# Local attention and a softplus FFN on one core: a hand-written issue order replaced by a list scheduler, with filler matmuls at the start

## Chip, cores and metric

The kernel runs on one core of a Trainium2 chip. The metric is the time of one execution on the device in microseconds (us); less is better. The profiler also gives the span, from the first to the last instruction, which is a little shorter.

## What is computed

Four batches, eight heads, 768 positions, head size 64. A query sees the first 8 keys of its batch and the 96 keys up to its own, with a bias that falls with the distance; softmax follows; the eight heads side by side are a row of 512 that goes through two matrices with a softplus between them:

```python
scores = scale * np.matmul(q, k.transpose(0, 1, 3, 2)) + bias[None, :, :, :]
scores = np.where(keep, scores, -1000000000.0)
a = np.exp(scores - np.max(scores, axis=-1, keepdims=True))
a = a / (np.sum(a, axis=-1, keepdims=True) + 1e-09)
attn_out = np.matmul(a, v)
x = attn_out.transpose(0, 2, 1, 3).reshape(B * S, H * D)    # 3072 x 512
h = x @ w_in                                                # w_in 512 x 2048
g = np.maximum(h, 0.0) + np.log1p(np.exp(-np.abs(h)))
out = g @ w_out                                             # w_out 2048 x 512
```

## The kernel before

**Units of work.** A *block* n (24 of them) is 128 positions of one batch with all heads. A *window* w (12) is two blocks: its q, k and v are loaded and transposed together. A *group* g (12) is the same 256 positions in the FFN. A group has eight *slots* p, each of two of the 16 chunks of the inner dimension.

**Attention of a window.** `load` (L96) fetches q, k, v in float32 on SyncE's queue, v in four pieces. `cast` (L114) makes bfloat16 of them (q on VectorE, k and v on GpSimd in most windows) and, for v, sets a column of ones with a memset (L130). `transp` (L133) has TensorE transpose q or k in eight steps into one PSUM bank `tr_ps` and copies them out on VectorE (L149).

**Attention of a block.** `scores` (L211) runs 16 small matmuls per half of the heads (8 in the first block of a batch) into `s_ps`, and VectorE adds the bias into `z` (L222). `expo` (L225) is ScalarE's exp. `pv` (L232) multiplies with v and the column of ones into `x_ps`, and VectorE normalizes into `xs` (L252, L253). `globals_k` on GpSimd (L160) and `globals_v` on VectorE (L167) copy the eight global keys and values into the neighbour block's tile, from block 2 of a batch on. `xs` then goes, transposed, to `XT`: for blocks 0 to 7 by TensorE and a copy (`x_transp`, L260), from block 8 on by a transposing DMA on SyncE's queue (`x_transp_dma`, L269). The first four blocks use `early_scores` (L191): there TensorE adds the bias, with matmuls of the bias by the identity (L196), and ScalarE reads PSUM directly. In these blocks the banks that later belong to the FFN serve as second banks for scores, for pv and for transposes (`s_alt`, `x_alt`, `tr_alt`, L399 to L402).

**FFN.** `mm1(g, p)` (L275) is eight matmuls of 256 columns into one of two banks `h_ps`, then an exp on ScalarE (L293) and, every second slot, one Ln with a bias of 1 over both slots (L295): softplus. `mm2(g, p)` (L302) is four matmuls of 512 columns into the two banks `o_ps`; after the last slot VectorE copies both banks (L316) and SyncE stores them (L320). `mm2` runs a group behind `mm1`.

**Weights.** `w_in_slice(s)` (L322) and `w_out_slice(s)` (L329) load a quarter of each matrix, with a cast to bfloat16, on GpSimd's DMA queue; a quarter serves two slots. `after_weights(s)` (L336) puts a tiny DMA on SyncE's queue that waits for a quarter of w_in, and so holds back the loads behind it.

**Order.** Every engine runs its instructions in the order in which the builder emits them. `at(t, fn, ...)` (L412) collects emissions with a time, and L544 sorts them. Up to about 49 us the times are written out one by one (L417 to L493); after that they follow from the block number, with a slot of 2.07 (L495 to L542). A `transp` emits its copy with it, a `scores` its bias add, a `pv` its normalization, an `mm1` its exp and Ln.

Of the kernel before, what the change touches and what calls it, by code (L numbers as in the profile page):

```python
# [12 lines left out]
BF16 = mybir.dt.bfloat16  # L13


@with_exitstack
def kernel(
# [19 lines left out]
    W = 2 * P  # L37
# [15 lines left out]
    GH = NG // 2  # L53

# [10 lines left out]
    ring = ctx.enter_context(tc.tile_pool(name="ring", bufs=5))  # L65
# [3 lines left out]

    s_ps = ps.tile([P, 8, P], F32, name="s_ps")  # L70
    x_ps = ps.tile([P, 512], F32, name="x_ps")
    tr_ps = ps.tile([P, 1024], BF16, name="tr_ps")
# [11 lines left out]

    state = {}

    def raw_tiles(w):
        if ("raw", w) not in state:
            state["raw", w] = (
                raw.tile([P, H, 2 * D], F32, tag="q32", name="q32"),  # L90
                raw.tile([P, H, 2 * D], F32, tag="k32", name="k32"),
                raw.tile([P, 2, H, D], F32, tag="v32", name="v32"),
            )
        return state["raw", w]

    def load(w, what, heads=slice(0, H)):  # L96
        b, ww = divmod(w, WPB)
        sl = slice(W * ww, W * ww + W)
        q32, k32, v32 = raw_tiles(w)
        if what == "v":  # L100
            for blk in range(2):
                t0 = W * ww + P * blk
                vv = v[b, :, t0 : t0 + P, :].rearrange("h (p r) d -> r p h d", r=2)
                for r in range(2):
                    nc.sync.dma_start(v32[64 * r : 64 * r + 64, blk, :, :], vv[r])  # L105
        else:
            dst, src = (q32, q) if what == "q" else (k32, k)
# [4 lines left out]
    cast_on = {"pool": nc.gpsimd.tensor_copy, "dve": nc.vector.tensor_copy, "act": nc.scalar.copy}  # L112

    def cast(w, which, eng, hs=slice(0, H)):  # L114
        q32, k32, v32 = raw_tiles(w)
        copy = cast_on[eng]
        if which in "qk":
            src = q32 if which == "q" else k32
            if (which + "b", w) not in state:
                state[which + "b", w] = qkv.tile(  # L120
                    [P, 2, H, D], BF16, tag=which + "b", name=which + "b"
                )
            copy(  # L123
                state[which + "b", w][:, :, hs, :],
                src[:, hs, :].rearrange("p h (r d) -> p r h d", r=2),
            )
        else:
            t = ring.tile([P, 2, H, D + 1], BF16, tag="vb", name="vb")
            copy(t[:, :, :, 0:D], v32[:])
            nc.gpsimd.memset(t[:, :, :, D : D + 1], 1.0)  # L130
            state["vb", w] = t

    def transp(w, which, psum, eng, ms=range(NPAIR)):  # L133
        src = state[which + "b", w]
        key = (which + "T", w)
        if key not in state:
            state[key] = (ring if which == "k" else qkv).tile(
                [P, 2, NPAIR, 2, 64], BF16, tag=which + "T", name=which + "T"
            )
# [9 lines left out]
        cast_on[eng](  # L149
            state[key][:, :, lo : lo + n, :, :].rearrange("p b m r t -> p b (m r) t"),  # L150
# [3 lines left out]
    def kt_of(n):  # L154
        return state["kT", n // 2][:, n % 2, :, :, :].rearrange("p m r t -> p m (r t)")

    def vb_of(n):
        return state["vb", n // 2][:, n % 2, :, :]
# [14 lines left out]
    def score_matmuls(n, half, banks, begin):  # L173

        i = n % NBLK
        qT = state["qT", n // 2][:, n % 2, :, :, :].rearrange("p m r t -> p m (r t)")
        for lh in range(4):
            h = 4 * half + lh
            m, sub = h // 2, h % 2
            rows = slice(64 * sub, 64 * sub + 64)  # L180
            for b in range(1 if i == 0 else 2):
                j = lh // 2 if i == 0 else 2 * (lh // 2) + b
                nc.tensor.matmul(  # L183
                    banks[lh % 2][:, j, :],
                    kt_of(n - b)[rows, m, :],
                    qT[rows, m, :],
                    start=begin,
                    stop=begin or (lh >= 2 and b == (0 if i == 0 else 1)),
                )

    def early_scores(n, half, banks):  # L191
# [11 lines left out]
        score_matmuls(n, half, banks, False)  # L203
        pb = work.tile([P, 8, P], BF16, tag="pb", name="pb")
        for e in range(2):
            nc.scalar.activation(  # L206
                pb[:, nr * e : nr * e + nr, :], banks[e][:, 0:nr, :], AF.Exp, scale=1.0 / root_d
            )
        state["pb", n, half] = pb

    def scores(n, half):  # L211
        score_matmuls(n, half, [s_ps[:, 0:4, :], s_ps[:, 4:8, :]], True)
        z = work.tile([P, 8, P], F32, tag="z", name="z")
# [9 lines left out]
        state["z", n, half] = z  # L223

    def expo(n, half):  # L225
        nr = 4 if n % NBLK == 0 else 8
        z = state.pop(("z", n, half))
        pb = work.tile([P, 8, P], BF16, tag="pb", name="pb")
        nc.scalar.activation(pb[:, 0:nr, :], z[:, 0:nr, :], AF.Exp, scale=1.0 / root_d)  # L229
        state["pb", n, half] = pb  # L230

    def pv(n, half, psum):  # L232
        i = n % NBLK
        pb = state.pop(("pb", n, half))
        if half == 0:
            state["xs", n] = work.tile([P, H, D], BF16, tag="xs", name="xs")
        xs = state["xs", n]
        xv = psum[:, 0 : 4 * (D + 1)].rearrange("p (h e) -> p h e", e=D + 1)
        for lh in range(4):
            h = 4 * half + lh  # L240
            j = perm.index(lh)
            if i == 0:
                nc.tensor.matmul(xv[:, lh, :], pb[:, j, :], vb_of(n)[:, h, :])
            else:
                nc.tensor.matmul(  # L245
                    xv[:, lh, :], pb[:, 2 * j, :], vb_of(n)[:, h, :], start=True, stop=False
                )
                nc.tensor.matmul(  # L248
                    xv[:, lh, :], pb[:, 2 * j + 1, :], vb_of(n - 1)[:, h, :], start=False, stop=True
                )  # L250
# [9 lines left out]
    def x_transp(n, psum, eng):  # L260
        xs = state.pop(("xs", n))
        tr = psum[:, 0:512].rearrange("p (m t) -> p m t", m=NPAIR)
        for m in range(NPAIR):
            nc.tensor.transpose(
                tr[:, m, :], xs[:, 2 * m : 2 * m + 2, :].rearrange("p a b -> p (a b)"), ident[:]
            )
        cast_on[eng](XT[:, :, P * n : P * n + P], tr)

    def x_transp_dma(n):  # L269
        xs = state.pop(("xs", n))  # L270
        nc.sync.dma_start_transpose(
            XT[:, :, P * n : P * n + P], xs[:].rearrange("p h d -> p (h d)")
        )

    def mm1(g, p):  # L275
        hv = h_ps[state["hslot"]][:].rearrange("p (j t) -> p j t", j=2)
        state["hslot"] ^= 1
# [10 lines left out]
        if p % 2 == 0:  # L288
            state["e", g] = ffn.tile([P, 2, 512], F32, tag="e", name="e")
        if p == 0:  # L290
# [290 lines left out]
```

## Time and profile before

| | us |
|---|---|
| median of 3 runs | 256.09 |
| the runs | 254.40, 256.09, 257.31 |
| profiled execution, its own time | 257.29 |
| its span | 255.5 |
| TensorE busy in it | 224.9 (88%) |
| ScalarE busy | 155.0 (61%) |
| VectorE busy | 125.1 (49%) |
| GpSimd busy | 36.3 (14%) |

The profiled execution took 1.79 us more than its span. Its own time lies 1.20 us above the median. Busy time is that of instructions; TensorE's matmuls overlap, and an end of a matmul is modelled, so spacing from start to start tells more than a duration.

### The profile page before, as it was taken

Reading aid. Unit: us, or ns where it says so; the run is one execution under the profiler, and the core shown is the slowest. Engines: PE = TensorE matmul, PEld = TensorE weight load, DVE = VectorE, ACT = ScalarE, POOL = GpSimd, SP = SyncE. Lnnn points to the kernel's source line nnn. Section 1 sums busy time; section 2 is a strip of 40 time slices with the busy share of each in tenths; the row PEclk is TensorE's granted clock in tenths of the full one; section 3 lists DMA queues with packets and bytes.
Section 4 is the critical chain, followed back from the end, with each engine's and each line's share of the span. In section 5 each row is a group of like instructions: output and inputs, shape, how many; then the busy total and the mean of one; then the engine's idle time right before and its main releaser. Section 6 shows DMA issues by size and latency. Waiting matters only on the chain.

```text
span 255.5 us, 5108 instructions
## 1 busy us (share of the span) xinstructions
PE 224.9 (88%) x2096; PEld 149.5 (59%) x2096; DVE 125.1 (49%) x259; ACT 155.0 (61%) x207; POOL 36.3 (14%) x68
## 2 busy tenths in 40 slices
PE   2759885977599799599999999999999999999991
PEld 1335664654367466367667766766676667666540
DVE  7263404664544666544555675745656656420102
ACT  3564576772705657447767776777677777776600
POOL 3370070030311000401000301301003000000000
PEclk9997999999959999889999999999999999999998
DMA  6979999928990305913653842844633213113033
GB/s 184 269 119 196 238 153 180 267 47 212 278 251 3 82 3 126 246 23 82 175 139 81 241 106 41 234 103 129 164 82 66 61 21 85 22 26 79 0 82 83
DMA packets 67193, 31.80 MB, mean 124 GB/s; under 512 B 35425, under 2 KB 64097, under 8 KB 67169
## 3 DMA queue, kind: packets, MB, share of 16 engines
q1 hardware_dynamic: 62944, 27.27, 42.7%
q0 software_dynamic: 4224, 4.19, 10.7%
q8 instruction: 16, 0.26, 0.4%
q14 instruction: 9, 0.07, 0.1%
HBM read 27.26 MB, written 6.29 MB: 131 GB/s over the span
## 4 chain that ended last, share of the span: by engine, by line
PE 80%; DMA 6%; DVE 4%; ACT 3%; issue 2%; SPq 2%; POOL 1%; DVEq 0%; POOLq 0%
PE h_psa L281 18%; PE o_psc L307 17%; PE h_psb L281 16%; PE o_psd L307 16%; PE s_ps L183 5%; PE tr_ps L144 4%; DMA w_in_bf<-in_moe_w_in_dram 3%; DMA XT<-xs 2%; ACT g L295 2%; DMA v_84<-in_v_dram 2%; PE x_ps L245 2%; PE x_ps L248 2%; DVE z L222 1%; ACT e L293 1%; SPq L105 1%
## 5 line engine op out<-in xcount | busy, mean ns | idle before, releaser
L281 PEld LDWEIGHTS <-w_in_bf 128*128 128x128 bf16 x768 | 73.2, 99 | 26.2 <-issue 3.9
L307 PE MATMUL o_psc<-w_out_bf,g 128*128 128x512 bf16 x192 | 58.5, 387 | 5.1 <-ACT g L295 4.8
L307 PE MATMUL o_psd<-w_out_bf,g 128*128 128x512 bf16 x192 | 57.8, 383 | 0.0
L307 PEld LDWEIGHTS <-g 128*128 128x128 bf16 x384 | 35.6, 99 | 35.1 <-ACT g L295 5.6
L281 PE MATMUL h_psa<-XT,w_in_bf 128*128 128x256 bf16 x384 | 51.9, 280 | 4.2 <-DMA XT<-xs 3.0
L222 DVE TENSOR_TENSOR z<-s_ps,biasA 128x1024 f32<-128x1024 f32 x34 | 41.5, 1221 | 22.5 <-PE s_ps L183 22.2
L293 ACT ACTIVATE e<-h_psb 128x512 f32<-128x512 f32 x48 | 28.6, 597 | 38.0 <-PE h_psb L281 38.0
L295 ACT ACTIVATE g<-e 128x1024 bf16<-128x1024 f32 x48 | 50.8, 1057 | 1.5
L281 PE MATMUL h_psb<-XT,w_in_bf 128*128 128x256 bf16 x384 | 50.0, 273 | 0.0
L293 ACT ACTIVATE e<-h_psa 128x512 f32<-128x512 f32 x48 | 28.4, 591 | 35.0 <-PE h_psa L281 34.8
L229 ACT ACTIVATE pb<-z 128x1024 bf16<-128x1024 f32 (+1 forms) x40 | 39.3, 982 | 1.9 <-DVE z L222 1.5
L252 DVE RECIPROCAL rcp<-x_ps 128x4 f32<-128x4 f32 x46 | 8.2, 178 | 30.7 <-PE x_ps L248 26.4
L316 DVE COPY osb<-o_psc 128x512 f32<-128x512 f32 x12 | 8.3, 691 | 26.2 <-PE o_psc L307 25.8
L253 DVE TENSOR_TENSOR xs<-x_ps,rcp 128x256 bf16<-128x256 f32 x46 | 19.5, 425 | 1.6
L165 POOL COPY kT<-kT 128x32 bf16<-128x32 bf16 x16 | 3.4, 213 | 116.0 <-PE s_ps L183 116.0
L183 PEld LDWEIGHTS <-kT 64*128 64x128 bf16 x352 | 10.5, 97 | 14.9 <-issue 11.5
L183 PE MATMUL s_ps<-qT,kT 64*128 64x128 bf16 x336 | 18.2, 225 | 1.0 <-DVE kT L149 0.6
L149 DVE COPY qT<-tr_ps 128x1024 bf16<-128x1024 bf16 (+1 forms) x12 | 7.8, 646 | 22.4 <-PE tr_ps L144 22.4
L245 PE MATMUL x_ps<-vb,pb 128*128 128x65 bf16 x156 | 15.0, 194 | 1.6 <-ACT pb L206 1.0
L144 PE MATMUL tr_ps<-ident,qb 128*128 128x128 bf16 x88 | 7.7, 235 | 8.9 <-POOL qb L123 5.0
L248 PE MATMUL x_ps<-vb,pb 128*128 128x65 bf16 x156 | 15.1, 194 | 0.0
L245 PEld LDWEIGHTS <-pb 128*128 128x128 bf16 x160 | 12.7, 99 | 2.8 <-ACT pb L206 1.3
(90 smaller groups left out, 149.4 us busy)
## 6 DMA issues: line engine op xcount, KB each, us to landing
out_dram<-osb SPq DMA_DIRECT2D x48, 128.0 KB, 2.4
w_in_bf<-in_moe_w_in_dram POOLq DMA_DIRECT2D x4, 512.0 KB, 7.3
w_out_bf<-in_moe_w_out_dram POOLq DMA_DIRECT2D x4, 512.0 KB, 9.7
q_82<-in_q_dram SPq DMA_DIRECT2D x2, 256.0 KB, 3.7
k_83<-in_k_dram SPq DMA_DIRECT2D x2, 256.0 KB, 4.1
v_84<-in_v_dram SPq DMA_DIRECT2D x4, 128.0 KB, 4.3
q_93<-in_q_dram SPq DMA_DIRECT2D x1, 512.0 KB, 4.9
k_94<-in_k_dram SPq DMA_DIRECT2D x1, 512.0 KB, 6.1
```

What stands on the lines that cost most here:

```text
L144: nc.tensor.transpose(tr[:, m - lo, r, :], src[:, r, 2 * m : 2 * m + 2, :].rearrange("p a b -> p (a b)"), ident[:],)
L183: nc.tensor.matmul(banks[lh % 2][:, j, :], kt_of(n - b)[rows, m, :], qT[rows, m, :], start=begin, stop=begin or (lh >= 2 and b == (0 if i ...
L222: nc.vector.tensor_tensor(z[:], s_ps[:], biasA[:, half, :, :], ALU.add)
L229: nc.scalar.activation(pb[:, 0:nr, :], z[:, 0:nr, :], AF.Exp, scale=1.0 / root_d)
L245: nc.tensor.matmul(xv[:, lh, :], pb[:, 2 * j, :], vb_of(n)[:, h, :], start=True, stop=False)
L248: nc.tensor.matmul(xv[:, lh, :], pb[:, 2 * j + 1, :], vb_of(n - 1)[:, h, :], start=False, stop=True)
L253: nc.vector.tensor_tensor(xs[:, 4 * half : 4 * half + 4, :], xv[:, :, 0:D], rcp[:][:, :, None].to_broadcast([P, 4, D]), ALU.mult,)
L281: nc.tensor.matmul(hv[:, j, :], w_in_bf[:, m, fb * P : fb * P + P], XT[:, m, W * g : W * g + W], start=(m == 0), stop=(m == NM - 1),)
L293: nc.scalar.activation(e[:, p % 2, :].rearrange("p (j t) -> p j t", j=2), hv, AF.Exp)
L295: nc.scalar.activation(state["g", g][:, 2 * p - 2 : 2 * p + 2, :].rearrange("p a t -> p (a t)"), e[:].rearrange("p a t -> p (a t)"), AF.Ln ...
L307: nc.tensor.matmul(o_ps[ns][:], gt[:, fb, ns * P : ns * P + P], w_out_bf[:, fb, :], start=(fb == 0), stop=(fb == NFB - 1),)
L316: nc.vector.tensor_copy(osb[:], o_ps[ns][:])
```

## The change

All work is described to a `Planner` as operations: engine (or a choice of engines), rough duration, what it comes after, the buffers that it takes and frees, and a rank. `plan` plays the program: whenever an engine is free in the play, it takes the operation of lowest rank whose inputs are done and whose buffers are free. The sequence so found is the order of emission. The play counts a result as seen 0.22 us after TensorE's end and 0.1 us after that of another engine, and models all DMAs as one pipe, first come, first served (1.85 us for q or k of a window, 2.45 for v, 3.1 for a weight slice, 0.65 for a transposing DMA, 0.7 to land). Semaphores are still placed by what an instruction reads and writes; the play decides the order alone.

With it: the functions are split, so that a copy, bias add, exp, Ln, normalization or store can stand elsewhere than right behind its matmuls. While TensorE has nothing ready before 24.0 in the play and bank pair O is free, a filler (identity by identity, 128 columns, into bank d) is emitted every 0.1. Weight slices 0 and 1 are planned from the landing of window 1's q on, slices 2 and 3 from that of window 2's q on; a DMA gate after slice 1 stands ahead of window 2's loads (as before) and one after slice 3, where it was slice 2, ahead of window 3's. Ranks put attention of block n (from 4 on) at 4n - 11 and `mm1` of group g at 8g, in slots. Blocks 6 and 7 use the transposing DMA. In the early blocks pv has one bank; q of window 1 is cast on GpSimd and k on ScalarE (before the other way round). The v tiles are five fixed ones, with their ones set once at the start. The last group's first output copy is on ScalarE. The arithmetic is the same.

The diff, cut; the removed functions and times are in the listing above:

```diff
--- before.py
+++ after.py
...
+    SEEN = {"pe": 0.22, "dve": 0.1, "act": 0.1, "pool": 0.1, "sp": 0.0}
...
+            for e in engine_free:
+                while engine_free[e] <= now:
+                    skipped, picked = [], None
+                    q = waiting[e]
+                    while q:
...
+                        if len(taken) == len(op.takes):
+                            picked = op
+                            break
+                        skipped.append(item)
...
+                    op = picked
+                    for b, slot in taken:
+                        self.rings[b][slot] = False
+                        self.turn[b] = (slot + 1) % len(self.rings[b])
+                    op.start, op.on, op.taken = now, e, taken
+                    engine_free[e] = op.end = now + op.engines[e]
+                    if op.dma is not None:
+                        first = now + 1.3 if e == "sp" else op.end + 1.2
+                        pipe = max(pipe, first) + op.dma
+                        op.end = pipe + 0.7
...
+                    left -= 1
+                    order.append(op)
+                    heapq.heappush(events, (engine_free[e], count, None, ()))
+                    heapq.heappush(events, (op.end + self.SEEN[e], count + 1, op, freed))
...
+                if e == "pe" and self.filler and engine_free[e] <= now < self.filler_until:
+                    if self.rings["O"][0]:
+                        f = Op("filler", "pe", 0.1, self.filler, 0.0)
+                        f.start, f.on, f.taken = now, "pe", []
+                        engine_free[e] = f.end = now + 0.1
+                        order.append(f)
+                        heapq.heappush(events, (f.end, count, None, ()))
+                        count += 1
...
-    events = []
-
-    def at(t, fn, *args):
-        events.append((t, len(events), fn, args))
...
-    at(14.0, w_in_slice, 0)
...
-    at(30.6, w_in_slice, 2)
...
-    T0, SLOT = 49.0, 2.07
-    start = {4: -6.5, 5: -4.5, 6: 0.8, 7: 2.8, 8: 7.0, 9: 10.0}
-    done_k, done_v = {3: 20.4}, {3: 22.0}
-    for n in range(4, NIT):
-        u = start.get(n, 4.0 * (n - 6) - 3.0)
...
+    def filler():
+        nc.tensor.matmul(alt["d"][:, 0:P], ident[:], ident[:])
+
+
+    pl = Planner(
+        {"S": 1, "X": 1, "TR": 1, "H": 2, "O": 1, "e": 3, "g": 3, "osb": 3, "z": 3, "pb": 3,
+         "xs": 3, "q32": 3, "k32": 3, "v32": 3, "qb": 2, "kb": 2, "qT": 2},
+        filler=lambda op: filler(),
+        filler_until=24.0,
+    )
...
+    def base(n):
+        return {0: -40.0, 1: -36.0, 2: -10.0, 3: -6.0}.get(n, 4.0 * n - 11.0)
...
+    def add_load(w, what, hs, rank, after=()):
+        nonlocal chain
+        part = 0.5 if hs != ALL else 1.0
+        dur, dma = (3.5, 2.45) if what == "v" else (0.55 * part + 0.05, 1.85 * part)
...
+        o = pl.add(
+            f"load{what}{w}", "sp", dur, lambda op: load(w, what, hs), rank,
+            after=[chain, *after], takes=takes, dma=dma,
...
+    def add_weights(s, rank, after=()):
+        landed_in[s] = pl.add(
+            f"w_in{s}", "pool", 0.78, lambda op: w_in_slice(s), rank, after=after, dma=3.1
+        )
...
+    add_load(0, "v", ALL, -190.0)
+    for i, what in enumerate("qkv"):
+        add_load(1, what, ALL, -180.0 + i)
+    add_weights(0, -170.0, [loaded[1, "q", 0]])
+    add_weights(1, -169.0, [loaded[1, "q", 0]])
+    gate = pl.add(
+        "gate1", "sp", 0.6, lambda op: after_weights(1), -160.0, after=[landed_in[1]]
+    )
+    for i, what in enumerate("qkv"):
+        add_load(2, what, ALL, -150.0 + i, [gate])
+    add_weights(2, -149.0, [loaded[2, "q", 0]])
+    add_weights(3, -148.0, [loaded[2, "q", 0]])
+    gate = pl.add("gate2", "sp", 0.6, lambda op: after_weights(3), -140.0, after=[landed_in[3]])
+    for w in range(3, NWIN):
+        for i, what in enumerate("qkv"):
+            add_load(w, what, ALL, base(2 * w) - 12.0 + i * (0.1 if w < 5 else 2.5), [gate])
+
...
+            else:
+                sc = pl.add(
+                    f"scores{n}{half}", "pe", pe,
+                    lambda op, half=half: scores(n, half, score_banks(op.taken), True), r,
+                    after=after, takes=(("S",),), frees=frees_q,
+                )
+                ab = pl.add(
+                    f"bias{n}{half}", "dve", 0.7 if i == 0 else 1.22,
+                    lambda op, half=half: add_bias(n, half), r + 0.1, after=[sc],
+                    takes=(("z",),), frees=[(sc, "S")],
+                )
+                ex = pl.add(
...
+            po = pl.add(
+                f"pv{n}{half}", "pe", 0.13 if i == 0 else 0.25,
+                lambda op, half=half: pv(n, half), r,
+                after=[exps[n, half], casts[w, "v"], gv.get(n),
+                       casts[prev // 2, "v"] if prev is not None else None],
...
+            xdone[n] = pl.add(
+                f"DX{n}", "sp", 1.2, lambda op: x_dma(n), u - 20.0, after=both,
+                frees=[(norm[n, 0], "xs")], dma=0.65,
...
+            r = float(NSLOT * g + p)
+            m1 = pl.add(
+                f"mm1_{g}_{p}", "pe", 0.875, lambda op, g=g, p=p: mm1(g, p, op.taken[0][1]), r,
+                after=[xdone[2 * g], xdone[2 * g + 1], landed_in[p * NS // NSLOT]],
...
+            r = p + 1.6 if g == 0 else NSLOT * (g + 1) + p + 0.5
+            mm2s[g, p] = pl.add(
+                f"mm2_{g}_{p}", "pe", 0.865, lambda op, g=g, p=p: mm2(g, p), r,
+                after=[lns[g, p // 2], landed_out[p * NS // NSLOT], mm2s.get((g, p - 1))],
...
+            oc = pl.add(
+                f"oc{g}_{ns}", "dve" if g < NGRP - 1 or ns else "act", 0.69,
+                lambda op, g=g, ns=ns: out_copy(op.on, g, ns), r - 2.0,
...
+    for t in vb_ring:
+        nc.gpsimd.memset(t[:, :, :, D : D + 1], 1.0)
+    plan = pl.plan({"pe": 2.4, "dve": 4.5, "act": 2.1, "pool": 3.2, "sp": 0.7})
+    for op in plan:
+        op.fn(op)
```

## Rows read from the trace of the kernel before

**Rows 1.** The page, 40 slices of 6.4 us: TensorE, its granted clock, DMA.

```profile
PE   2759885977599799599999999999999999999991
...
PEclk9997999999959999889999999999999999999998
DMA  6979999928990305913653842844633213113033
```

**Rows 2.** Busy time by stretch: length, PE (x) PEld DVE ACT POOL, PEclk, DMA share, GB/s.

```profile
120.00:140.00 20.00, 20.00 (x194) 13.73 (x192) 11.20 (x22) 13.38 (x19) 1.21 (x3) 1.00 0.47 123
```

**Rows 3.** The chain that ended last, in order of time: start, length, what.

```profile
14.22 6.62 DMA w_in_bf<-in_moe_w_in_dram
...
68.56 1.49 DVE qb L123
...
101.44 5.55 DMA XT<-xs
...
110.41 0.87 PE h_psb L281 x8
111.28 0.45 PE tr_ps L144 x8
...
144.98 0.87 PE h_psb L281 x8
...
214.57 0.87 PE h_psb L281 x8
...
226.59 0.87 PE h_psb L281 x8
...
228.33 0.87 PE h_psa L281 x8
```

**Rows 4.** Timeline of the end: the last matmuls and output copies.

```profile
249.21 0.59 PE L307 MATMUL o_psd<-w_out_bf,g 128*128 128x512 bf16 x2
249.41 0.69 DVE L316 COPY osb<-o_psc 128x512 f32<-128x512 f32 x1 [6.29 <-PE o_psc L307]
250.02 0.68 DVE L316 COPY osb<-o_psd 128x512 f32<-128x512 f32 x1
```

**Rows 5.** Busy time by stretch, around three falls of TensorE's clock; columns as in rows 2.

```profile
22.00:25.00 3.00, 3.00 (x28) 1.82 (x27) 1.30 (x5) 1.27 (x3) 0.00 (x0) 0.54 1.25 205
70.00:76.00 6.00, 5.90 (x38) 3.74 (x39) 2.18 (x7) 0.60 (x1) 0.40 (x2) 0.50 1.03 268
104.00:107.00 3.00, 0.01 (x1) 0.00 (x0) 1.78 (x5) 1.57 (x2) 1.06 (x3) 0.95 1.18 266
107.00:110.00 3.00, 2.98 (x12) 1.66 (x12) 0.00 (x0) 0.60 (x1) 0.26 (x1) 0.50 0.23 61
```

**Rows 6.** Waits, longest first in total: us, times, longest.

```profile
PE tr_ps L144 <- DVE qb L123: 3.9, 2, 2.9
...
PE o_psc L307 <- ACT g L295: 4.8, 4, 1.8
PE h_psa L281 <- DMA XT<-xs: 3.0, 1, 3.0
```

**Rows 7.** Timeline of GpSimd: start, duration, line, operation, idle before and its releaser.

```profile
3.67 0.61 POOL L123 CAST qb<-q_82 128x512 bf16<-128x512 f32 x1 [1.44 <-DMA q_82<-in_q_dram]
...
9.28 1.05 POOL L129 CAST vb<-v_84 128x1024 bf16<-128x1024 f32 x1 [1.92 <-DMA v_84<-in_v_dram]
...
13.24 1.04 POOL L123 CAST kb<-k_94 128x1024 bf16<-128x1024 f32 x1 [2.81 <-DMA k_94<-in_k_dram]
14.22 0.89 POOL L325 DMA_DIRECT2D w_in_bf<-in_moe_w_in_dram  x1
...
26.77 0.21 POOL L165 COPY kT<-kT 128x32 bf16<-128x32 bf16 x1 [6.21 <-PE s_ps L183]
...
33.25 0.75 POOL L325 DMA_DIRECT2D w_in_bf<-in_moe_w_in_dram  x1
...
68.34 1.04 POOL L129 CAST vb<-v_823 128x1024 bf16<-128x1024 f32 x1 [2.07 <-DMA v_823<-in_v_dram]
```

**Rows 8.** Groups by line and shape: busy us, mean ns, idle before; a memset, the same cast twice.

```profile
L130 POOL MEMSET vb<- 128x16 bf16 x12 | 2.6, 215 | 0.0
...
L123 DVE CAST qb<-q_821 128x1024 bf16<-128x1024 f32 x1 | 1.6, 1562 | 0.0
...
L123 DVE CAST qb<-q_850 128x1024 bf16<-128x1024 f32 x1 | 0.7, 685 | 0.0
```

**Rows 9.** DMA issues: line, count, KB each, median us to landing.

```profile
w_in_bf<-in_moe_w_in_dram POOLq DMA_DIRECT2D x4, 512.0 KB, 7.3
...
k_564<-in_k_dram SPq DMA_DIRECT2D x1, 512.0 KB, 11.3
...
k_822<-in_k_dram SPq DMA_DIRECT2D x1, 512.0 KB, 5.0
```

**Rows 10.** Timeline of TensorE, start and duration: four transposes early, eight later.

```profile
4.33 0.61 PE L144 MATMUL tr_ps<-ident,qb 128*128 128x128 bf16 x4 [4.33 <-POOL qb L123]
...
59.55 0.61 PE L144 MATMUL tr_ps<-ident,kb 128*128 128x128 bf16 x8 [0.52 <-DVE XT L267]
```

**Rows 11.** Timeline of the bias add and of the scores that wait for its bank.

```profile
46.92 1.23 DVE L222 TENSOR_TENSOR z<-s_ps,biasA 128x1024 f32<-128x1024 f32 x1 [3.73 <-PE s_ps L183]
...
48.20 0.40 PE L183 MATMUL s_ps<-qT,kT 64*128 64x128 bf16 x8
```

More of the change, by code (lines that the diff above doesn't have):

```diff
@@ L171, in globals_v, with score_banks, bias_in @@
             nc.vector.tensor_copy(vb_of(n - 1)[sl, :, 0:D], vb_of(first)[sl, :, 0:D])
[L173 to L191, printed above, removed]
+    def score_banks(taken):
+        if taken[0][0] == "S":
+            return [s_ps[:, 0:4, :], s_ps[:, 4:8, :]]
+        return [alt[x][:].rearrange("p (j t) -> p j t", j=4) for x in "ab"]
+    def bias_in(n, half, banks):
         nr = 2 if n % NBLK == 0 else 4
@@ L202, in early_scores, with scores, add_bias @@
             )
[L203 to L213, printed above, removed]
+    def scores(n, half, banks, begin):
+        i = n % NBLK
+        qT = qk_of("q", n)
+        for lh in range(4):
+            m, sub = (4 * half + lh) // 2, lh % 2
+            rows = slice(64 * sub, 64 * sub + 64)
+            for b in range(1 if i == 0 else 2):
+                nc.tensor.matmul(
+                    banks[sub][:, lh // 2 if i == 0 else 2 * (lh // 2) + b, :],
+                    qk_of("k", n - b)[rows, m, :],
+                    qT[rows, m, :],
+                    start=begin,
+                    stop=begin or (lh >= 2 and b == (0 if i == 0 else 1)),
+                )
+    def add_bias(n, half):
+        z = tile_of(work, ("z", n, half), [P, 8, P], F32)
         if n % NBLK == 0:
@@ new lines @@
+    EARLY = 4
+    ALL = slice(0, H)
+    halves = ((slice(0, 4), range(0, 2)), (slice(4, H), range(2, NPAIR)))
+    whole = ((ALL, range(NPAIR)),)
+    def base(n):
+        return {0: -40.0, 1: -36.0, 2: -10.0, 3: -6.0}.get(n, 4.0 * n - 11.0)
+    loaded, chain = {}, None
+    def add_load(w, what, hs, rank, after=()):
+        nonlocal chain
+        part = 0.5 if hs != ALL else 1.0
+        dur, dma = (3.5, 2.45) if what == "v" else (0.55 * part + 0.05, 1.85 * part)
+        takes = ((what + "32",),) if (w, what, 0) not in loaded else ()
+        o = pl.add(
+            f"load{what}{w}", "sp", dur, lambda op: load(w, what, hs), rank,
+            after=[chain, *after], takes=takes, dma=dma,
+        )
+        loaded[w, what, 0 if hs == ALL or hs.start == 0 else 1] = o
+        if hs == ALL:
+            loaded[w, what, 1] = o
+        return o
@@ new lines @@
+    landed_in, landed_out = {}, {}
+    def add_weights(s, rank, after=()):
+        landed_in[s] = pl.add(
+            f"w_in{s}", "pool", 0.78, lambda op: w_in_slice(s), rank, after=after, dma=3.1
+        )
+        landed_out[s] = pl.add(
+            f"w_out{s}", "pool", 0.78, lambda op: w_out_slice(s), rank + 0.01, after=after, dma=3.1
+        )
+    for hs, _ in halves:
+        for what in "qk":
+            add_load(0, what, hs, -200.0 + len(loaded))
+    add_load(0, "v", ALL, -190.0)
```

558 lines of the change are left out of this document (334 added, 224 removed), and 5 rows, old and new, of the table events.

## The prediction

> **What bounds the kernel now.** The page's slices come first [rows 1]. Read TensorE's line against the DMA line: from slice 18 on (about 110 us) TensorE shows 9 in every slice but the last, and DMA about a third; before that TensorE dips again and again while DMA is at 9 or 0 in turn. So there are two stages: a ragged one up to about 110 us, and a dense one.
>
> The table by stretch settles the dense stage: TensorE busy 20.00 of 20.00 us at a granted clock of 1.00, ScalarE at 13.4, VectorE at 11.2 [rows 2]. TensorE is the bound there, and no order of issue can shorten it. The chain gives its pace [rows 3]: the same matmul group of four windows' distance starts at 144.98 and at 214.57, so one window costs 69.59 / 4 = 17.40 us. Near the end, with no attention left, two neighbouring mm1 start 228.33 - 226.59 = 1.74 us apart: a slot of mm1 and mm2. Eight slots are 13.9 us, and 17.4 - 13.9 = 3.5 us is attention, per window.
>
> All of TensorE's work at that pace is 12 x 17.40 = 208.8, and the early stage adds the bias matmuls of blocks 0 to 3 (twelve of 512 and four of 256 columns; a matmul of 512 takes a quarter of mm2's 1.74 - 0.87 us, 0.217: 3.0 us) and, by TensorE, six transposes of X (four steps each, where eight take 0.45 [rows 3]: 1.3 us; before there are eight of them, 0.4 more). Sum 213.1 us. The last matmul ends at 249.8 [rows 4], and from 110.4 on [rows 3] TensorE is dense: 139.4 us. So 213.1 - 139.4 = 73.7 us of work had been done by 110.4, and 36.7 us were lost. That loss is what the change can reach.
>
> Where it lies: nothing runs on TensorE before 4.3 us [rows 10]. The chain's longest piece of DMA, the first slice of w_in, lands at 20.84 (14.22 + 6.62) [rows 3]. Three times TensorE's clock falls to its lower level (0.50, 1.2 instead of 2.4 GHz) after a thin stretch: around 22 to 25, 70 to 76 and 107 to 110 us [rows 5], some 12 us, which cost half, 6 us. The wait list adds single stalls [rows 6]: q's cast 2.9, the transposing DMA of X 3.0 (the chain shows 5.55 for it [rows 3]), and four waits of mm2 for Ln, 4.8 together. These waits have one pattern: the instruction at TensorE's head waits, while others that are ready stand behind it.
>
> **The change, part by part.** *Order.* The work is the same; nearly everything else is a move. I price it by asking when TensorE can become dense, and what it has done by then.
>
> GpSimd decides when weights start. In the kernel before, w_in slice 0 is issued at 14.22, behind the cast of window 1's k; after the change it stands behind the cast of window 0's v, which ends at 10.33 [rows 7]. The issue moves up by 3.9 us, and slots 0 and 1 can start near 17 to 18 instead of 20.9. The price: q of window 1 is now cast on GpSimd behind four weight issues of 0.75 to 0.89 us [rows 7], so from about 13.6 to 14.6; k, which GpSimd had cast by 14.28 [rows 7], goes to ScalarE. About equal, so 0; without the early weights it would be a gain of some 3 us at window 1. The twelve memsets of v's ones (0.215 us each [rows 8]) become five, 1.1 us ahead of GpSimd's first cast, inside the 1.44 us that it waits for q anyway [rows 7]: 0. One pv bank instead of two delays X of blocks 0 and 1 by up to two normalizations, 1.2 us, hidden because w_in is later still.
>
> Blocks 2 and 3 remain a chain through one scores bank; globals_k of block 4, before at 26.77 [rows 7], ends it. Behind it GpSimd issues slices 2 and 3, with no real wait in front: at 27 instead of 33.25. With 5 to 10 us to landing (median 7.3 [rows 9]) w_in slice 2 is there at 32 to 37 us; I take 35. Up to then there is work for: attention of two windows, 2 x 3.5 + 3.0 = 10.0 us, and what slices 0 and 1 allow, mm1 of groups 0 and 1 and mm2 of group 0, four slots each: 12 x 0.87 = 10.4 us. Together 20.4 of 35 us; the scheduler can't lose less without data.
>
> From there on: 213.1 - 20.4 = 192.7 us remain. Between 35 and 45 us the rest of the weights and window 2 arrive. Work for that time is mm1 on slice 2 (4 x 0.87), mm2 on slice 2 (1.7), attention of window 2 (3.5) and mm1 of group 2: 12 us for 10, so nearly dense. I allow 2 us of misfit (bounds 0 and 6, the latter if window 2 comes as late as k_564 did).
>
> *Fillers.* Up to bank pair O's first use (about 21 us) the idle time of TensorE is filled, some 80 to 110 matmuls. Four early transposes took the 0.61 us in which eight ran later, although the granted clock reads 1.00 [rows 10]; warm, a filler takes about 0.055 us, less than the 0.1 of the play, so they don't delay the work behind them. What they can bring is a first stage at the upper level and no fall at 22 us, a few us of TensorE time, but that stage ends with the arrival of weights. I take 0; bounds: a gain of 1.9 us (half of the first fall), a loss of 1 us.
>
> After 24 us there are no fillers, and the wait for slice 2 can bring one more fall, as the waits before 70 and 107 us did [rows 5]. Half of the 3 us at 107 is 1.5 us; I charge it once (bounds 0, and 3.0 by half of the fall from 70 to 76). The Trainium skill, TensorE: Matmul & The Clock Gate, section HAM oscillation, says that each long enough wait for DMA sends the array back to half rate, and that work must be packed to keep it warm. The falls at 70 and 107 agree; by it a filler that stops early buys nothing, and by the rows the term stays 1.5.
>
> *The steady part.* The order now comes from rough times. Where the play is late against the chip, nothing is lost; where it is early, TensorE waits. The cast of q is 0.69 in the play and 0.685 in the group list, though one took 1.562 [rows 8]. After a bias add that ends at 48.15 the scores start at 48.20 [rows 11], a delay of 0.05 where the play counts 0.1. So the play errs to the safe side; I charge 1 us (bounds 0, and ten late casts of 0.88 us, 8.8).
>
> *Small ones.* Blocks 6 and 7 by DMA save TensorE two transposes (counted above). Their DMA may take 5.55 us [rows 3], but attention is ranked 11 slots, 19 us, ahead of its group, and X is done some five slots into that, so about 10 us cover it; with less than three slots left it would show. The last two copies, at 249.41 and 250.02 [rows 4], now run on two engines: 0.6 us off the tail of 255.5 - 249.8 = 5.7.
>
> **Sum**: 35 + 192.7 + 2 + 1.5 + 1 = 232.2 for TensorE's end, + 5.1 tail = 237.3 of span, + 1.8 outside = 239.1 against the profiled 257.3: 18 us less. That execution is 1.2 above the median of 256.1, so a median of 238.
>
> **Rivals.**
>
> *A, dense at once.* Slice 2 lands at 33, no misfit, no fall, no late casts: 33 + 192.7 + 5.1 + 1.8 - 1.2 = 231.4. For it: the delays are on the safe side. Against it: DMA stands mostly at 9 up to 50 us [rows 1], so the second weights can hardly come sooner.
>
> *B, plan too tight.* TensorE's queue holds each transpose just where the play has q ready, and GpSimd's casts fall on VectorE's in each of ten windows: 238 + 8.8 = 247. For it: the cast of 1.562 us, at 68.56 [rows 3], ran beside GpSimd's at 68.34 [rows 7]. Against it: only one of ten was hit before.
>
> *C, blocked by loads: slower.* The play treats DMA as one line served in order. On the chip GpSimd's and SyncE's transfers share: k_564, loaded beside weight slices, took 11.3 us against 5.0 for a lone k_822 [rows 9], where the play allows 5.7 from issue of q. If the transposes of a window stand at TensorE's head when planned, while FFN work waits behind, that costs 5.6 us. In windows 2 to 5 it is 22.4 and the time 238 + 22.4 = 260; it passes 256 from 4.5 us per window on. Against it: the gate behind slice 3 keeps the loads of windows 3 to 5 off the weights. The Trainium skill, DMA: Bandwidth & Descriptors, section Issuing engines are not separate DMA queues, states the same sharing whatever engine issues; by it window 2 is late, which is within my misfit, and the other three only if stores and transposing DMAs do likewise.
>
> *D, the change doesn't do what it says.* The order that comes out is much like the written one, for the arrival of weights sets the first 50 us either way and slots fill as before; only the falls at 70 and 107 and the wait for X go: 4.9 + 3.0, half of that kept: 252.
>
> **Chances.** Forecast (233.5 to 243) 0.50, A 0.15, B 0.15, D 0.12, C 0.08. The predicted time is 238. The range 231 to 249 takes in A and B and leaves out D and C, 0.2. This kernel's measurement can tell about 1%, 2.6 us: faster by more 0.87 (forecast, A, B and 0.07 of D), within 1% 0.05 (the rest of D), slower 0.08 (C).
>
> **What would show it.** Right: w_in slice 0 issued near 10.5 and slices 2 and 3 near 27 us; TensorE's slices at 9 from about 38 us on, mean work per window still 17.4; no wait of TensorE of over 2 us after 45; the granted clock at 1.00 from then. Wrong: dips between 45 and 110 us with a transpose or pv waiting for a cast or a load (B or C), a clock of 0.5 there, a window longer than 17.4 in the dense stage, or slices 2 and 3 landing after 45.

## The result, and the profile after

| | before | after |
|---|---|---|
| median, us | 255.51 (254.40 to 257.31, 4 runs) | 249.00 (246.74 to 251.51, 4 runs) |
| profiled execution, its span | 257.29, 255.5 | 246.74, 245.0 |
| TensorE busy in it | 224.9 | 225.4, 93 fillers among it |

The ratio is 0.9661, 95% interval 0.9557 to 0.9765: faster. In a later set, with more runs, the changed kernel took 250.96 (247.62 to 252.88, 10 runs) beside 254.31 for the kernel before, ratio 0.9872 (0.9815 to 0.9929). The ratios leave disturbed runs out, so they are not the ratio of the medians. By the two ratios the gain is 8.7 and 3.3 us, and not 18: 1 to 4%. The changed kernel's runs lie 2% apart, which has to be explained too.

The page of the changed kernel, 40 slices of 6.1 us, beside [rows 1]:

```profile
PE   6887989999996999598999999999999999999990
...
PEclk9999999999999999799999999999999999999999
DMA  6999899999999999999602303213113114021033
```

Up to slice 11 TensorE is as forecast, and so is its clock. Then come three dips, and the DMA line has changed its shape: it stands at 9 from the first slices to slice 18 (116 us) and is nearly empty behind that, where before it went up and down as windows were loaded. The same by stretch, columns as in [rows 2]:

```profile
42.00:116.00 74.00, 67.08 (x664) 45.32 (x662) 44.33 (x87) 48.15 (x64) 16.15 (x20) 0.98 1.09 225
...
100.00:104.00 4.00, 3.33 (x16) 2.39 (x17) 0.00 (x0) 1.41 (x2) 3.01 (x3) 0.58 1.08 279
```

In 74 us TensorE lacks 6.9, and the DMA engines are busy all the time (1.09) at 225 GB/s. The wait list, beside [rows 6], gives nearly all of the lack to one cause:

```profile
PE h_ps L414 <- DMA XT<-xs: 6.3, 3, 2.9
```

The first matmuls of groups 3, 4 and 5 wait for X of blocks 7, 9 and 11, which the transposing DMA brings. The chain, beside [rows 3], has the three, from issue to landing, and the clock fall behind the second: sixteen matmuls of 256 columns in 3.54 us, otherwise in 1.75, so 1.8 us more:

```profile
72.44 6.16 DMA XT<-xs
...
96.78 3.84 DMA XT<-xs
100.67 3.54 PE h_ps L414 x16
...
110.18 5.42 DMA XT<-xs
...
239.38 0.69 DVE osb L452
```

To read one of them in full, take X of block 7 through four views. VectorE's timeline has its normalization end at 66.65. SyncE's has its DMA issued only at 72.44, behind the loads of two later windows. TensorE's has the matmul start at 78.65 after 2.35 us of idleness:

```profile
66.23 0.42 DVE L382 TENSOR_TENSOR xs<-x_ps,rcp 128x256 bf16<-128x256 f32 x1
```

```profile
67.47 0.51 SPq L244 DMA_DIRECT2D k_1084<-in_k_dram  x1
68.08 3.42 SPq L241 DMA_DIRECT2D v_1103<-in_v_dram  x4
71.55 0.80 SPq L244 DMA_DIRECT2D q_1158<-in_q_dram  x1
72.44 1.98 SPq L404 DMA_TRANSPOSE XT<-xs  x1
```

```profile
78.65 1.59 PE L414 MATMUL h_ps<-XT,w_in_bf 128*128 128x256 bf16 x13 [2.35 <-DMA XT<-xs]
```

So block 7 was normalized 76.30 - 66.65 = 9.7 us before TensorE wanted its X. X then spent 5.8 us in SyncE's queue and 6.2 us from issue to landing. Blocks 9 and 11 read the same way: VectorE has two normalizations per block, and the second of each ends at 87.39 and 108.86; the chain above has the issues, at 96.78 and 110.18.

```profile
86.97 0.42 DVE L382 TENSOR_TENSOR xs<-x_ps,rcp 128x256 bf16<-128x256 f32 x1
...
108.44 0.42 DVE L382 TENSOR_TENSOR xs<-x_ps,rcp 128x256 bf16<-128x256 f32 x1
```

So they spent 9.4 and 1.3 us in the queue and 3.8 and 5.4 us from issue to landing. All transposing DMAs of this kernel, by their line:

```profile
DMA to landing us min/median/max: 2.4/2.7/6.2
```

Why the loads stand there: the play serves whatever can run. A load can run as soon as one of three raw buffers is free, and a cast, which frees one, as soon as its load is in. So in 74 us all windows from 3 on are loaded, up to five ahead of their use. The last v is issued at 112.18; in the kernel before, whose loads were spaced by hand with the blocks, at 183.60. SyncE's timelines, first of after, then of before:

```profile
112.18 2.74 SPq L241 DMA_DIRECT2D v_1726<-in_v_dram  x4
```

```profile
183.60 2.72 SPq L105 DMA_DIRECT2D v_2305<-in_v_dram  x4
```

### The profile page after: what moved, and what is told of

Same layout as the page of the kernel before. It is cut to its first block, busy times and chain, and to the rows that moved or that the text cites. A ratio compares the mean times of both kernels' runs of the same rounds, so it can differ in the third digit from the quotient of the medians.

```text
span 245.0 us, 5282 instructions
## 1 busy us (share of the span) xinstructions
PE 225.4 (92%) x2181; PEld 154.1 (63%) x2181; DVE 123.5 (50%) x256; ACT 153.3 (63%) x208; POOL 35.5 (14%) x61
## 4 chain that ended last, share of the span: by engine, by line
PE 78%; DMA 10%; SPq 5%; DVE 4%; issue 1%; ACT 1%; DVEq 0%
PE h_ps L414 34%; PE o_ps L442 31%; DMA XT<-xs 6%; PE s_ps L326 5%; DMA v_208<-in_v_dram 4%; PE x_ps L370 3%; PE tr_ps L267 3%; SPq L241 3%; SPq L244 2%; DVE osb L452 1%; DVE z L344 1%; ACT g L428 0%; PE tr_ps L392 0%; PE s_ps L310 0%; PE alt_d L526 0%
## 5 line engine op out<-in xcount | busy, mean ns | idle before, releaser
L414 PE MATMUL h_ps<-XT,w_in_bf 128*128 128x256 bf16 x768 | 98.5, 276 | 6.3 <-DMA XT<-xs 6.3
L442 PE MATMUL o_ps<-w_out_bf,g 128*128 128x512 bf16 x384 | 97.2, 380 | 0.9 <-ACT g L428 0.5
L424 ACT ACTIVATE e<-h_ps 128x512 f32<-128x512 f32 x96 | 55.9, 590 | 40.4 <-PE h_ps L414 40.0
L452 DVE COPY osb<-o_ps 128x512 f32<-128x512 f32 x23 | 15.6, 686 | 24.3 <-PE o_ps L442 23.9
L370 PEld LDWEIGHTS <-pb 128*128 128x128 bf16 x320 | 14.9, 98 | 7.7 <-issue 1.6
L326 PEld LDWEIGHTS <-kT 64*128 64x128 bf16 x352 | 10.2, 94 | 10.4 <-issue 8.7
L526 PE MATMUL alt_d<-ident 128*128 128x128 bf16 x93 | 9.1, 247 | 2.3 <-POOL ident masks.py:199 2.3
L526 PEld LDWEIGHTS <-ident 128*128 128x128 bf16 x93 | 6.9, 112 | 3.2 <-POOL ident masks.py:199 2.3
L276 DVE COPY kT<-tr_ps 128x1024 bf16<-128x1024 bf16 x11 | 7.5, 685 | 2.5 <-PE tr_ps L267 2.5
L267 PEld LDWEIGHTS <-kb 128*128 128x128 bf16 x96 | 6.1, 100 | 2.3 <-ACT kb L256 0.5
L356 ACT ACTIVATE pb<-s_ps 128x512 bf16<-128x512 f32 (+1 forms) x12 | 5.6, 524 | 2.9 <-PE s_ps L326 2.9
```

The source lines that it names most:

```text
L267: nc.tensor.transpose(tr[:, m - lo, r, :], src[:, r, 2 * m : 2 * m + 2, :].rearrange("p a b -> p (a b)"), ident[:],)
L326: nc.tensor.matmul(banks[sub][:, lh // 2 if i == 0 else 2 * (lh // 2) + b, :], qk_of("k", n - b)[rows, m, :], qT[rows, m, :], start=begin, ...
L370: nc.tensor.matmul(xv[:, lh, :], pb[:, 2 * j + b, :], vb_of(n - b)[:, h, :], start=b == 0, stop=b == 1,)
L414: nc.tensor.matmul(hv[:, j, :], w_in_bf[:, m, fb * P : fb * P + P], XT[:, m, W * g : W * g + W], start=(m == 0), stop=(m == NM - 1),)
L424: nc.scalar.activation(e[:, p % 2, :], state["h", g, p][:], AF.Exp)
L442: nc.tensor.matmul(state["o", g][ns][:], gt[:, fb, ns * P : ns * P + P], w_out_bf[:, fb, :], start=(fb == 0), stop=(fb == NFB - 1),)
```

## The experiments

Twelve runs in three sets of four, each set on a chip of its own, with its own runs of the kernel before. Theory 1: X's transposing DMA, and casts, are late because loads that run ahead fill SyncE's queue (1a) and the DMA engines (1b). Theory 2 began as "window 3 arrives late, and attention with it", and became "the order is built on landing times that the chip doesn't reach".

| run | what differs from the changed kernel | median, us | ratio to before, 95% |
|---|---|---|---|
| e1_tx14 | X of blocks 6 to 13 by TensorE | 243.19 | 0.9613 (0.9580 to 0.9647) |
| e2_hold | q of windows 5 on held | 248.99 | - |
| e3_nofill | no fillers | 249.30 | 0.9819 (0.9765 to 0.9874) |
| e4_actdx | X's DMA on ScalarE's queue | 249.99 | 0.9873 (0.9807 to 0.9938) |
| h0_after | nothing | 250.96 | 0.9872 (0.9815 to 0.9929) |
| g1_hold3 | q, k and v of windows 5 on held | 238.83 | 0.9430 (0.9341 to 0.9519) |
| g3_tx14_hold3 | the same, and X as in the first | 242.76 | 0.9642 (0.9529 to 0.9754) |
| g4_tx14_lag | X as in the first; the play has loads land later | 240.81 | 0.9550 (0.9456 to 0.9643) |
| k0_hold3 | as g1 | 239.65 | 0.9465 (0.9408 to 0.9523) |
| j1_hold3_nofill | g1 without fillers | 238.73 | 0.9392 (0.9335 to 0.9450) |
| j2_hold3_latew | g1, weights as late as before | 240.84 | 0.9498 (0.9443 to 0.9553) |
| j5_hold3_w2late | g1, w_out 2 and slice 3 behind v of window 2 | 242.16 | 0.9568 (0.9514 to 0.9622) |

### Without the transposing DMA, with less fillers, on another queue

**e1_tx14.**

```diff
-        if n < 6:
+        if n < 14:
```

> X of blocks 6 to 13 goes through TensorE instead of the transposing DMA. Theory 1 (the DMA of X is late because loads run ahead of it): the three waits of mm1 for XT, 6.3 us, and the clock fall behind the second, 1.8 us, go; eight more transposes of X cost TensorE 1.8 us; profiled span about 239 instead of 245.0, time about 241. Theory 2 (attention itself is late, because window 3 lands only at 53 us): the same waits turn up before the TensorE transposes or behind them, in all 4 us or more, and the time stays within 2 us of the changed kernel.

243.19, 6 to 7 us under e3 and e4 on the same chip. The changed kernel itself wasn't run on that chip, and the interval overlaps that of its first set. The waits for X are gone, but TensorE has new ones, 2.3 us, behind VectorE. VectorE's timeline shows why:

```profile
75.33 0.69 DVE L276 COPY qT<-tr_ps 128x1024 bf16<-128x1024 bf16 x1 [0.53 <-PE tr_ps L267]
79.06 0.69 DVE L256 CAST qb<-q 128x1024 bf16<-128x1024 f32 x1 [3.05 <-DMA q<-in_q_dram]
79.67 0.17 DVE L381 RECIPROCAL rcp<-x_ps 128x4 f32<-128x4 f32 x1
79.88 0.42 DVE L382 TENSOR_TENSOR xs<-x_ps,rcp 128x256 bf16<-128x256 f32 x1
```

VectorE stands 3.05 us before the cast of a late q, and a normalization that could have run stands behind it; TensorE waits for that one. The cast itself is not urgent: TensorE next transposes a q at 96.76, and this one at 114.38. So the transposing DMA was not the only way in which late loads reach TensorE.

**e2_hold**, for w from 5 on:

```diff
+        loaded[w, "q", 0].after.append(norm[2 * (w - 2) + 1, 1])
```

> Loads of window 5 and later are placed on SyncE's queue behind the transposing DMA of the second block two windows earlier, so they no longer run ahead. Theory 1: X lands 2.4 to 3.5 us after its issue instead of up to 6.2, issue follows the normalization within 1 us, mm1 waits for XT under 2 us in all; span about 239 to 240, time about 241. Theory 2: no gain, and windows 5 and 6 come later, so the time is the same or up to 3 us more.

248.99 (244.30 to 250.72), and two waits for X of 5.0 us together. This hold was half a hold: k and v of the same windows still ran ahead, and they are two thirds of the bytes. The waits stayed, so it doesn't bear Theory 1 out; and with most of the bytes still running ahead it doesn't speak against it.

**e3_nofill** (`filler_until=0.0`).

> No fillers. What the prediction took (fillers are worth nothing, because the weights' arrival ends that stage): granted clock falls to its lower level once around 20 to 25 us, time within 1.5 us of the changed kernel. If fillers carry part of the gain: 2 us or more slower. Theories 1 and 2 say nothing on it: the waits for XT stay.

249.30, within the changed kernel's runs; with the stalls on X in it (8.3 us), it can't tell what fillers are worth. k0 and j1 below can.

**e4_actdx**: `nc.scalar.dma_start_transpose`, planned on ScalarE.

> The transposing DMA is issued from ScalarE's queue, loads stay where they are. Theory 1a (X waits on SyncE's queue behind the loads' issue): X of block 7 is issued within 1 us of its normalization, not 5.8 us after it; waits for XT fall under 3 us, time 3 to 5 us less. Theory 1b (X shares the DMA engines with loads in flight): it still takes 5 us or more to land, and the time falls by less than 2 us. Theory 2: no change.

249.99, no better. There is no queue of loads in front of X now, yet the landing is the slowest of all runs:

```profile
DMA to landing us min/median/max: 2.4/3.2/8.5
```

But no matmul waits for X any more. TensorE loses the time elsewhere: behind an exp of ScalarE, and behind output copies that wait for stores.

```profile
PE o_ps L442 <- DVE osb L452: 2.6, 2, 2.3
PE h_ps L414 <- ACT e L424: 2.6, 1, 2.6
```

ScalarE's timeline has the reason for the second: X's DMA now stands in ScalarE's queue, and what is behind it waits with it, here 5.46 us. The normalization that this X needs stands on VectorE behind the cast of a late q.

```profile
89.64 1.87 ACTq L404 DMA_TRANSPOSE XT<-xs  x1
91.56 1.06 ACT L428 ACTIVATE g<-e 128x1024 bf16<-128x1024 f32 x1 [5.46 <-DVE z L344]
```

So 1a isn't the whole cause: with another queue and the loads as dense, other late loads take the time. It isn't refuted either, for the waits on X went; and since the play's order changed with the edit, the run doesn't say how the stalls divide between queue and engines. The Trainium skill, DMA: Bandwidth & Descriptors, section Issuing engines are not separate DMA queues, says that transfers of all issuers interleave on the same DMA engines and that a second issuer saves only issue time. The 8.5 us agree.

### Holding the loads

**h0_after**, the changed kernel again.

> The changed kernel once more, as the measure for the other three of this job. Both theories: 246.7 to 251 us as at first, waits of TensorE for the transposed X of 5 us and more, and DMA busy in nearly every slice up to 116 us.

250.96; three waits for X, 7.4 us.

**g1_hold3**, for w from 5 on and each of q, k, v:

```diff
+            loaded[w, what, 0].after.append(norm[2 * (w - 2) + 1, 1])
```

> q, k and v of window w, from 5 on, may be loaded only after block 2w - 3 is normalized; X of blocks 6 and on still goes by the transposing DMA. Theory 1 (loads that run up to five windows ahead fill the DMA engines and SyncE's queue, and X's transposing DMA waits in that crowd): the DMA slices between 60 and 116 us fall from 9 to some 5, X lands 2.5 to 4 us after its issue, the waits for it fall from 6.3 us to under 1.5, and the time is 238 to 242. Theory 2 (not the crowd: the order is built on landing times that the chip never reaches, however little is under way): X and q still come 3 us and more later than the order has them, waits of 4 us and more stay, 245 to 249.

238.83 beside 250.96 on the same chip, 11 to 12 us less (by the ratios and by the medians), and TensorE waits for X not once. Its page, then the landing of its transposing DMAs, then the stretch in which the changed kernel had its dips:

```profile
PE   6886979799999999999999999999999999999990
...
PEclk9999999999999999999999999999999999999998
DMA  5999899999419419519439239249259015030033
```

```profile
DMA to landing us min/median/max: 2.4/2.6/3.9
```

```profile
60.00:116.00 56.00, 55.05 (x549) 38.37 (x557) 35.13 (x65) 39.04 (x52) 8.22 (x12) 1.00 0.62 135
```

The DMA line shows one window at a time: a 9, then a 4 and a 1. In all it moves the bytes that the changed kernel moves, but in this stretch at 135 GB/s, where that one has 225 in its 74 us, and TensorE is dense from 60 us on. The hold acts through the order on SyncE's queue, where the loads of a window now stand behind the DMA of X:

```profile
78.43 8.74 SPq L404 DMA_TRANSPOSE XT<-xs  x2
87.23 0.58 SPq L244 DMA_DIRECT2D q<-in_q_dram  x1
```

This is Theory 1 with its numbers, and the strict form of Theory 2 (late however little is under way) falls. The hold empties the queue (1a) and the engines (1b) at once, so the two stay unseparated.

**g3_tx14_hold3**, both edits.

> The same hold, and X of blocks 6 to 13 transposed by TensorE. Theory 1: what was left in the run without the hold (q of window 7 late, VectorE standing behind its cast) goes too: 239 to 241; but with no transposing DMA in SyncE's queue the loads are held by the order alone, so they may still run ahead some. Theory 2: as without the hold, 243 to 244.

242.76, more than Theory 1's 239 to 241 and just under Theory 2's 243 to 244; yet its profiled execution has a span of 239.0, no wait for X and none for q. Against g1 it gives TensorE eight more transposes of X. At four steps each (half of the 0.45 of [rows 3]) they are 8 x 0.22 = 1.8 us, just the difference of the spans, 239.0 - 237.2. Under a hold the transposing DMA is the better place for them. Why its other runs lie higher still is open.

**g4_tx14_lag**: the traffic is left as it is, and the play alone is told later landings.

```diff
-                        op.end = pipe + 0.7
+                        op.end = pipe + 0.7 + getattr(op, "lag", 0.0)
```

> X of blocks 6 to 13 by TensorE, no hold; the play alone is told that loads land later: window 2's v by 8 us, those of windows 3 and on by 4 us each. The traffic stays as dense. Theory 1: DMA still at 9 up to about 115 us, stalls behind late casts of q or v stay, 243 to 245. Theory 2: the casts stand later in the order, VectorE no longer waits on q at 72 to 79 us, TensorE waits under 1 us in all after 50 us, 240 to 241.

240.81, which is Theory 2's number, with the DMA line as Theory 1 has it:

```profile
DMA  6999699999999899999103113113114015031033
```

The stall on q is gone. The two theories name two ends of one gap: a stall needs a load that lands late and an order that counted on it early. Closing the second end took away the stall on q, with X by TensorE; for X's DMA it wasn't tried. Against e1, on another chip, the intervals overlap, so the size of this cure (0.6% by the ratios) isn't settled.

### What the other terms are worth, with the loads held

**k0_hold3** is g1 again.

> The changed kernel with q, k and v held (from window 5 on, until block 2w - 3 is normalized), once more, as the measure for the other three of this job: 237.6 to 241.9 us, median near 239.

239.65, as expected. **j1_hold3_nofill** (`filler_until=0.0`):

> The held kernel without filler matmuls. Theory 1 (fillers keep the clock up, but that stage ends with the arrival of weights): the granted clock reads 0.8 to 0.9 before 20 us, and the time is within 1 us of the held kernel. Theory 2 (they are part of the gain): the early attention runs at half the clock, slots 0 and 1 start later, and the time is 2 to 3 us more.

238.73, no worse than with fillers. By stretch, first without, then with them (k0):

```profile
0.00:10.00 10.00, 4.99 (x40) 2.77 (x40) 5.65 (x27) 5.20 (x10) 3.12 (x15) 1.00 0.85 194
10.00:20.00 10.00, 6.89 (x76) 4.79 (x75) 4.27 (x13) 4.73 (x8) 5.29 (x7) 0.77 1.24 225
```

```profile
0.00:10.00 10.00, 6.83 (x70) 5.14 (x71) 5.68 (x27) 4.80 (x9) 3.03 (x15) 1.00 0.87 187
10.00:20.00 10.00, 7.43 (x118) 5.85 (x117) 4.27 (x13) 5.07 (x9) 5.29 (x7) 1.00 1.25 217
```

Fillers do lift the mean granted clock of the second stretch from 0.77 to 1.00, and VectorE does the same work in it either way, 4.27 us. That fits an early stage that runs at the pace of its loads (DMA 1.24 and 1.25), not of TensorE.

**j2_hold3_latew**: slices 0 and 1 planned behind the cast of q of window 1, slices 2 and 3 behind that of v of window 2.

```diff
+            op.after.append(casts[1, "q", 0] if s < 2 else casts[2, "v"])
```

> The held kernel with the weights planned about where the kernel before had them: slices 0 and 1 behind the cast of window 1's q, slices 2 and 3 behind the cast of window 2's v. Theory 1 (the arrival of slice 2 sets when TensorE becomes dense): slices 2 and 3 are issued 6 us or more later than at 28 to 31 us, TensorE becomes dense that much later, partly filled with other work, and the time is 3 to 6 us more: 242 to 245. Theory 2 (window 2's attention sets it, and its v comes sooner with no weights beside it): v of window 2 lands before 38 us and the time is within 1 us of the held kernel.

240.84 beside 239.65, intervals overlapping: Theory 2, near enough. GpSimd's timeline has v of window 2 cast at 34.95, and only then the weights:

```profile
34.95 1.04 POOL L253 CAST vb<-v 128x1024 bf16<-128x1024 f32 x1 [1.25 <-DMA v<-in_v_dram]
35.94 0.74 POOL L464 DMA_DIRECT2D w_in_bf<-in_moe_w_in_dram  x1
```

In the changed kernel the same engine has them the other way round:

```profile
28.71 0.74 POOL L464 DMA_DIRECT2D w_in_bf<-in_moe_w_in_dram  x1
...
41.58 1.04 POOL L253 CAST vb_88<-v_537 128x1024 bf16<-128x1024 f32 x1 [7.40 <-DMA v_537<-in_v_dram]
```

Weights 7 us sooner cost v 6.6 us; against k0, where they stand at 29.46 and 43.03, it is 6.5 us for 8.1. With DMA full, the early stage can choose which of the two comes first, and the choice is worth 1.2 us by the medians, which the noise covers.

**j5_hold3_w2late**: w_in slice 2 stays, the other three wait for the cast of v of window 2.

> The held kernel with w_in slice 2 where it was, and w_out slice 2 and both parts of slice 3 behind the cast of window 2's v. Theory 1 (v of window 2 is late because it shares the DMA engines with four weight transfers): v lands at 34 to 38 us instead of 42.5, TensorE's waits for its cast (1.3 us twice) go, 237 to 238. Theory 2 (v's small pieces are slow by themselves): v still lands after 41 us, the rest of the weights come that much later, and the time is 1 to 4 us more.

v is cast at 37.68 in place of 43.03, so it was late by sharing, as Theory 1 says; and yet 242.16, as Theory 2 says. The gate behind slice 3 lands later with the weights, so q of window 3 is issued at 47.77 and not at 44.02, and TensorE waits 2.1 us for its cast. What one load gained the next one lost.

## Why the prediction was wrong, point by point

**The sum** came out for a kernel in which loads don't run ahead, which is not the one that it was made for. It gave 237.3 of span; g1 and k0 have 237.2 and 237.1, and medians of 238.83 and 239.65 against 238. The steady window is still 17.4 us, and TensorE is dense from 36 us on, to the first stall. Some of that is luck, for within the sum small errors cancel. The clock fall (1.5) doesn't come in g1. The weights were issued 1.0 and 1.7 us later than I had them (11.52 and 28.71 in place of 10.5 and 27). And the tail gave nothing: in the changed kernel TensorE's last matmul ends as the last copy starts, at 239.38 (the chain above), 5.6 us before the end, where I had 5.1 and the kernel before 5.7 [rows 4].

**The step that failed** is "Small ones": "attention is ranked 11 slots, 19 us, ahead of its group, and X is done some five slots into that, so about 10 us cover it", set against a DMA that "may take 5.55 us". Both halves fail, and the step looked at blocks 6 and 7 alone; of the three that stalled, 9 and 11 went by DMA before as well.

- *The price.* From the end of the normalization to landing it was 12.0 us for block 7, 13.2 for block 9 and 6.7 for block 11; from block 12 on, with few loads left, it was 2.4 to 3.0. I took the 5.55 as what such a DMA costs, and it was what it had cost in one crowd, from issue on. I never asked what stands in front of it on SyncE, though the change replaced that whole order.
- *The cover.* The 11 slots are the rank of a group's first block. `mm1` also waits for the second, n = 2g + 1, ranked at 4n - 11 = 8g - 7: seven slots ahead, and its last pv 4.3 slots into them. So fewer than three slots are left, and the prediction itself says that this would show. In g1, where the order isn't bent by late loads, block 7 is normalized at 68.15 and the first matmul of group 3 starts at 72.77, 4.6 us later. There X lands 2.4 us after the normalization, so the thin cover holds:

```profile
67.73 0.42 DVE L382 TENSOR_TENSOR xs<-x_ps,rcp 128x256 bf16<-128x256 f32 x1
```

```profile
72.77 1.91 PE L414 MATMUL h_ps<-XT,w_in_bf 128*128 128x256 bf16 x16
```

In the changed kernel TensorE wanted X 9.7, 10.4 and 5.8 us after the normalization, but that is no cover. The play had seen the crowd too. Played over, the listing has X land 9.5, 10.4 and 5.3 us after the normalization, and puts the matmul right behind: block 7's X at 75.30, the matmul at 75.69. A rank says who goes first among those that are ready; it keeps no distance. On the chip these DMAs took 2.4, 2.9 and 1.4 us more than in the play, and TensorE waited 2.35, 2.93 and 1.04. An order without slack turns each late landing into a stall.

The price in TensorE's time: 6.3 us of waits and 1.8 of the clock fall are 8.1, and 245.0 - 237.3 is 7.7. The spread of the changed kernel's runs belongs here as well: where a stall is a race of a DMA against a matmul, it differs by execution. It has 6.3 us of these waits in one profile and 7.4 in another; that the slowest runs have more of them is likely, and wasn't profiled.

**"Where the play is late against the chip, nothing is lost; where it is early, TensorE waits."** True, but I went over compute alone (casts, bias adds), where the play does err to the safe side, and left its DMA model to rival C. There I looked for late loads of windows 2 to 5, and put against it that the gate keeps them off the weights. It does; they crowd each other and X instead. I wrote that C holds "only if stores and transposing DMAs do likewise". Transposing DMAs did, and the step that I didn't take was to ask what sets the time of a load: in the kernel before a list of times, in the new one a free buffer. Playing the listing before the run would have shown it.

**Terms that held.** Fillers 0: j1. Window 2's misfit 2: v of window 2 was cast at 41.58 where the play has its load landed at 33.55; TensorE waited 1.3 us for it in g1 and not at all in the changed kernel's profile. Memsets, pv's bank and q's cast on GpSimd: in the changed kernel's profile the longest wait of TensorE that could be put down to one of them is 0.6 us (`x_ps` behind the normalization).

**A reason that was wrong though its number fitted.** I let the arrival of slice 2, at 35 us, say when TensorE becomes dense, and had slots 0 and 1 start some 3 us sooner for slice 0. j2 takes both back for 1.2 us. What is left for the gain over the kernel before is the order itself, with fewer instructions at TensorE's head that wait while others could run [rows 6]; no run tests that by itself.

**Rivals.** B's 247 is near the measured time by another mechanism: in the changed kernel no transpose waits for a cast for more than 0.3 us. C's mechanism came, at a third of its price and from another direction. D's 252 is near the second set's 250.96, but the order that came out was not like the old one.

## What to carry to other kernels

A list scheduler that never leaves a queue idle starts every transfer at the first moment that its buffer is free; where DMA is scarce in one stage and idle in the next, tie each load to the use that it serves (here: no sooner than two windows ahead), which gave 11 to 12 us here for a loop of four lines. When a change replaces an order, ask of each queue what now stands in front of the few instructions that are late most easily, and take a duration measured in one crowd as that crowd's. And a rank is no lead: read the slack out of the plan before counting on it.

## What the runs showed of the hardware

- A transposing DMA of 128 x 512 takes 2.4 us from issue to landing with little beside it, and 6.2, 7.1 and 8.5 us at most where the engines are full. Issuing slows as well: 1.2 us for it in the quiet, up to 2.4 in the crowd; the load of a q or k, 0.5 us in the quiet, took 2.73 in h0_after.
- The clock didn't fall behind the longest of the three DMA chains. After 2.35 us of idleness at 76 us the stretch stays at 1.00; after 2.93 us at 98 us TensorE ran at its lower level (0.58 on the mean of 100 to 104 us). In e4 it ran at the lower level behind a wait of 2.62 us (0.50 on the mean of 93 to 97 us; in the four us before TensorE was busy for 0.65).
- A granted clock of 0.77 in the second 10 us, in j1, cost nothing that can be measured, which fits a stage that waits for loads.
